# Pooled attention and gated feed-forward: queries of sequences 4 and 5 turned by DMA, eleven late buffers, new orders

## The chip, the cores and the metric

The kernel runs on one core of one Trainium2 chip. The metric is the device time of one execution in microseconds. Before the change it is 210.57 us, the median of three runs (210.29 to 210.69).

## The reference

Eight sequences of 576 tokens, eight heads of 64. Keys and values are averaged over groups of 8 tokens (72 of each are left), queries attend to them, and the result of all heads (512 columns) goes through a gated feed-forward: a product, a convolution of three taps along the tokens, a sigmoid gate, a second product.

```python
k_p = k.reshape(B, H, Sp, pool, D).mean(axis=3)
v_p = v.reshape(B, H, Sp, pool, D).mean(axis=3)
scores = scale * np.matmul(q, k_p.transpose(0, 1, 3, 2))
...
attn = np.exp(scores - max); attn = attn / attn.sum()
x = np.matmul(attn, v_p)            # then (B, S, H * D)
h = np.maximum(x @ w_in, 0.0)
conv_out = sum(conv_w[k] * hp[:, k:k + S, :] for k in range(3))
out = h * sigmoid(conv_out) @ w_out
```

The sums of the second half are shortened here; `scale` is 1/8, `w_in` 512 x 1024, `w_out` 1024 x 512. Inputs and output are float32; the kernel computes in bfloat16 with float32 sums.

## The kernel before

**Work.** The sequences stand in four groups of two: group g holds sequences 2g and 2g + 1. A group's tokens are cut into tiles of 128 rows (tile 4 has 64 of each sequence; group 0 has ten tiles, with 64 rows each of tiles 4 and 9). For each sequence: load queries, keys and values (GpSimd's queue, POOL, which casts float32 to bfloat16 on the way), pool keys and values on VectorE (DVE), turn the keys and the queries so that the head dimension lies on the partitions. For each tile: scores on TensorE (PE, line 608 or 621), maximum (DVE, 634), shift, exponential (ScalarE, ACT, 683), turn of the weights, product with the values (PE, 718), division by the sum (`att_divide`: on ACT eight instructions at line 739, one for each head, or on DVE one at line 746), turn of the result. For each sequence: the first product (`ffn_in`, PE, 776; eight blocks of two halves, each half four matmuls), relu (ACT, 785), the convolution either on PE (940) or as two taps on DVE (912), sigmoid or tanh (ACT), gates (DVE, 990), and the second product for each tile (`ffn_out`, PE, 998; two halves of four matmuls), copied to a buffer (1009) and stored (1021).

**Two ways to turn.** The weights of groups 2 and 3 and the attention results of these groups are turned by a DMA that transposes, issued by SyncE's queue (SP): `att_send` (702, eT<-e) and `att_out` (755, xT<-x). The queries of sequences 0 to 5 are turned on PE: `prep_q`, per sequence two half-turns, either 18 matmuls in the half form (line 542) or 36 in the quarter form (546), and each is copied from PSUM to `qT` by ACT or DVE (560). Where `Q_DMA` names the group (before: group 3 alone), `add_prep_q` instead adds one `q_send` (line 553), a DMA on SP from `qp` to `qT`. Then the keys are laid out otherwise: `turn_keys` (494), once for each sequence, writes the turned keys to both halves of the partitions and `copy_keys` (505) copies them once; in the other groups `turn_pair` (471) turns both sequences' keys together and `copy_pair` (484) copies them in four parts. Scores of a group in `Q_DMA` are always in the quarter form (32 small matmuls, line 608); elsewhere `FORMS` picks that or four full ones (621).

**Order.** Nothing is decided at run time. `Graph.add` makes a list of operations in a fixed sequence of code; `ORDER` lists them by twice their number plus one if the second possible engine takes it, and -1 stands for a fill, a matmul without use. The engines' queues are in this order: each engine takes its own entries one after the other and waits at each for what it needs. So a position in `ORDER` says what is queued behind what. `FORMS` gives the shape of those operations that have two, `PLACES` the buffer or PSUM bank of each use.

**Buffers.** `qT` has three buffers, `qp` (queries as loaded) four, `v` three, `kk` (keys as loaded) one. A load waits until its buffer's last reader is done, and all later loads wait behind it in POOL's queue. The output tiles of group 3 go to "late" buffers: the four `qp` buffers, cut in halves, are read as eight buffers of float32. `add_out` lets their first writer wait until the queries of sequences 4 to 7 are turned:

```python
half_qp = [t.rearrange("p h s -> p (h s)")[:, i * 1024:(i + 1) * 1024] for t in buffers["qp"] for i in range(2)]
buffers["late"] = [t.bitcast(FP32) for t in half_qp]
```

Of the kernel before, what the change touches and what calls it, by code (L numbers as in the profile page):

```python
# [33 lines left out]
class Graph:  # L34
# [23 lines left out]
    Q_DMA = (3,)  # L58
# [14 lines left out]
        0, 16, 4, 24, 12, 44, 28, 8, 10, 14, 32, -1, -1, 42, 36, -1, -1, 40, -1, -1,  # L73
        2, -1, 38, -1, 66, 64, -1, -1, 19, 68, -1, 48, 21, -1, 60, -1, -1, 46, 102, 7,
        26, 34, 114, 118, 106, 116, 121, 108, 104, 113, 111, 122, 126, 125, 292, 128, -1, 74, 30, 294,
        358, -1, -1, 70, 360, 296, -1, -1, 298, 50, 362, 364, 336, 338, 58, 314, 300, 316, 340, -1,
        -1, 342, 130, -1, 318, -1, 344, 320, 132, 380, 303, 134, 322, 382, 347, 194, 196, 136, 384, 201,
        324, 72, 348, 386, 326, 199, 350, 366, 352, 78, 304, 369, 328, 206, 306, 330, 202, 209, 308, 370,
        204, 388, 354, 391, 372, -1, 548, 374, 310, 332, 550, 313, 392, 357, 394, 552, 396, 526, 554, 376,
        528, 398, 335, 570, 556, 401, 572, 530, 226, 532, 558, 574, 379, 228, 230, 576, 504, 444, 506, 84,  # L80
        233, 446, 62, 138, 508, 448, 482, 438, 510, 140, 440, 142, 426, 56, 442, 534, 428, 484, 432, 430,
        144, 434, 537, 52, 486, 76, 512, 488, 420, 436, 422, 514, 80, 560, 54, 424, 516, 402, 562, 518,
        564, 414, 416, 520, 404, 418, 466, 406, 210, 472, 470, 468, 212, 578, 566, 474, 408, 568, 476, 410,
        580, 478, 238, 412, 456, 241, 480, -1, 458, 450, 460, 214, 538, 452, 522, 540, 454, 542, 234, 525,
        462, -1, -1, 237, 582, 216, 262, 221, 584, 464, 82, 225, -1, -1, 219, -1, 223, -1, -1, 265,
        978, 586, 544, 490, 980, 547, 770, 588, 592, 982, 591, 493, 772, 748, 984, 594, 750, 600, 774, 597,
        752, 776, 258, 146, 494, 261, 602, 496, 148, 498, 1000, 605, 934, 608, 1002, 754, 150, 500, 1004, 778,
        503, 610, 936, 781, 756, 152, 613, 624, 759, 154, 626, 614, 86, 1006, -1, 938, 760, 642, 628, 156,
        90, 644, 940, 762, 158, 956, 764, 646, 1008, 942, 958, 94, 1011, 704, 630, 945, 706, 98, 632, 960,
        636, 22, 634, 638, 708, 672, 640, 160, 962, 242, 1012, 96, 676, -1, 782, 674, 986, 1014, 784, -1,  # L90
        88, 1016, 989, 792, 766, 794, 710, 654, 656, 786, 769, 1018, 796, 658, 964, 990, 967, 244, 946, 660,
        1021, 992, 948, 994, 662, 798, 968, 950, 664, 788, 800, 970, 791, 246, 678, 972, 803, 162, 248, 680,
        804, 682, 164, 92, 974, 255, 806, 666, 808, 257, 253, 668, 251, 166, 977, 810, 168, 1186, -1, 670,
        952, 1188, 100, 996, 813, -1, -1, 1190, 999, 694, 955, 170, 1204, 696, 1096, 1206, 1098, 698, 172, 726,
        1192, 1060, 1208, 1100, 1062, 728, 712, 1064, 648, 174, 730, 715, 650, 1090, 176, 652, 1092, 684, 732, 1168,
        688, 1094, 1170, 1104, 1072, 690, 1074, 178, 692, 270, 1076, 1172, 716, 273, 1066, 700, 1194, 1068, 1174, 616,
        1070, 718, 1176, 686, 618, 721, 1084, 180, -1, 702, 1086, 621, -1, 1088, 1150, 1140, 1152, 1210, 1078, 1118,
        1142, 1212, 1080, 1144, 1124, 266, 1082, 1154, 1054, 606, 269, 1102, 1056, 1120, 1196, 1058, 622, 734, 1126, 1428,
        737, 1222, 1198, 830, 1430, 1156, 290, 1224, 1201, 814, 1432, 816, 1226, 1128, 1178, 274, 738, 1122, 832, 819,
        740, 182, 722, 1180, 820, 838, 742, 725, 1182, 835, 744, 840, 1106, 747, 1184, 276, 1410, 843, 1134, 1412,  # L100
        1228, 1158, 884, 1136, 1108, 886, 1138, 1112, 1214, 1230, 888, 878, 1216, 1110, 1414, 880, 1446, 1218, 882, 872,
        1448, 874, 1434, 1220, 918, 278, 876, 1450, 890, 288, 922, 1146, 892, 920, 1160, 894, 846, 1162, 1114, 1165,
        860, 1148, 866, 1436, 868, 1116, 862, 184, 1166, 870, 848, 1130, 864, 280, 1132, 851, 1232, 1202, 283, 284,
        1234, 908, 287, 1236, 1676, 186, 1238, 910, 854, 912, 1678, 1438, 856, 1452, 1440, 836, 1680, 896, 858, 898,
        1442, 1416, 1454, 1640, 188, 902, 900, 1642, 1316, 190, 906, 1644, 1418, 1318, 904, 192, 1392, 1320, 924, 1394,
        1444, 1646, 1322, 1396, 928, 1324, 926, 914, 1280, 1326, 1456, 1398, 1282, 1334, 1458, 930, 1292, 1461, 1400, 1286,
        1288, 1382, 1294, 1648, 1284, 1304, 916, 1296, 1306, 1290, 1462, 1298, 1308, 932, 1300, 1328, 1682, 1402, 1310, 844,
        1302, 1404, 1384, 1312, 1407, 1330, 822, 1336, 1684, 824, 1342, 1314, 1408, 1338, 1604, 827, 1332, 1658, 1420, 1660,
# [1391 lines left out]
```

## Time and profile before

| | |
|---|---|
| median of three runs | 210.57 us (210.29, 210.57, 210.69) |
| the profiled execution | 210.06 us |
| its span, first to last instruction | 208.3 us |
| granted clock of TensorE, mean | 0.993 |
| DMA moved | 33.48 MB, 161 GB/s mean |
| HBM read | 32.52 MB |

The profile is of one execution on the one core. PE is TensorE's matmuls, PEld its weight loads, DVE VectorE, ACT ScalarE, POOL GpSimd, SP SyncE; an engine's name with q is its queue. Groups name a line of the kernel, the output tile and the inputs, the shapes and the count, then busy us, mean ns of one, and the idle time just before them with what ended most of it. The chain of waits is followed back from the last instruction, at each step to what released it; its rows are start, length, and what ran. DMA rows give the issuing queue, the size where it is known, and the median time from issue to landing; queue q0 holds POOL's loads, q1 what SP issues. Rows of a table by stretches give the stretch, its length, then the busy time and number of instructions of PE, PEld, DVE, ACT and POOL, the granted clock, the busy share of the 16 DMA engines and GB/s.

### The profile page before, as it was taken

To read this page: it belongs to the slowest core of one execution; us is meant where nothing else is said; L and a number is where in the kernel's file an instruction comes from. 1 tells how busy PE (TensorE), PEld (TensorE's weight loads), DVE (VectorE), ACT (ScalarE), POOL (GpSimd) and SP (SyncE) were. 2 spreads that over 40 slices of the span, in tenths; PEclk is the share of its full clock that TensorE was granted. 3 is DMA by queue.
4 is the path that set the end of the run, shared out by engine and by line. 5 is a ranking of instruction groups with operands and counts; after the bars stand their busy time and mean duration, and the time that the engine had idled before them with its cause. 6 is when DMAs were issued, how large, how long until landed. Compare 5 with 4: busy or idle time off the path is not lost.

```text
span 208.3 us, 6540 instructions
## 1 busy us (share of the span) xinstructions
PE 197.2 (95%) x2650; PEld 134.3 (64%) x2666; DVE 190.4 (91%) x338; ACT 174.5 (84%) x363; POOL 45.5 (22%) x74
## 2 busy tenths in 40 slices
PE   4999999999999999999999999999999999999990
PEld 2568688776688887666868875566556666644450
DVE  7979999889999999999999999999999999999440
ACT  3558786998899999998998999999999999797310
POOL 8553035010173211010000152040234315000000
PEclk9999999999999999999999999999999999999997
DMA  6999999999999999998497465565665557044395
GB/s 205 243 204 209 205 207 208 208 209 203 189 167 202 205 207 206 170 162 164 92 144 123 97 136 111 119 138 127 129 139 116 120 124 179 3 101 102 92 282 185
DMA packets 48835, 33.48 MB, mean 161 GB/s; under 512 B 28300, under 2 KB 43812, under 8 KB 48804
## 3 DMA queue, kind: packets, MB, share of 16 engines
q0 software_dynamic: 15216, 15.40, 45.1%
q1 hardware_dynamic: 32592, 16.20, 36.4%
q10 hardware_dynamic: 996, 1.45, 2.6%
q8 instruction: 21, 0.34, 0.6%
q14 instruction: 10, 0.08, 0.1%
HBM read 32.52 MB, written 9.44 MB: 201 GB/s over the span
## 4 chain that ended last, share of the span: by engine, by line
PE 49%; DVE 24%; ACT 16%; issue 5%; DMA 3%; SPq 0%; DVEq 0%; ACTq 0%
PE psum L776 19%; PE psum L998 13%; DVE tg L912 6%; DVE negm L634 4%; ACT x L739 4%; PE psum L718 3%; DVE gT L990 3%; DVE sd L646 3%; DMA hT<-in_k_dram 3%; PE psum L940 2%; ACT hT L785 2%; PE psum L693 2%; PE psum L608 2%; ACT gT L922 2%; ACT qT L560 2%
## 5 line engine op out<-in xcount | busy, mean ns | idle before, releaser
L776 PE MATMUL psum<-xT,w_in_sb 128*128 128x288 bf16 x512 | 70.6, 286 | 0.4
L998 PE MATMUL psum<-w_out_sb,gT 128*128 128x512 bf16 (+1 forms) x280 | 65.9, 373 | 1.1 <-issue 0.2
L776 PEld LDWEIGHTS <-w_in_sb 128*128 128x128 bf16 x512 | 48.4, 98 | 15.6 <-issue 0.6
L785 ACT ACTIVATE hT<-psum 128x576 bf16<-128x576 f32 x64 | 41.6, 671 | 4.8 <-PE psum L776 4.2
L998 PEld LDWEIGHTS <-gT 128*128 128x128 bf16 x296 | 27.7, 98 | 27.5 <-DVE gT L990 0.6
L860 POOL COPY hT<-hT 128x126 bf16<-128x126 bf16 x14 | 11.3, 810 | 84.2 <-issue 43.6
L912 DVE SCALAR_TENSOR_TENSOR tg<-hT,ratio 128x576 f32<-128x576 bf16 x36 | 28.2, 813 | 0.5 <-ACT gT L922 0.2
L634 DVE TENSOR_REDUCE negm<-psum 128x8 f32<-128x576 f32 (+2 forms) x37 | 27.4, 748 | 1.3 <-PE psum L608 0.6
L912 DVE SCALAR_TENSOR_TENSOR tg<-hT,ratio,tg 128x576 f32<-128x576 bf16 x36 | 28.2, 810 | 0.0
L922 ACT ACTIVATE gT<-tg,ratio 128x576 bf16<-128x576 f32 x36 | 27.4, 793 | 0.8 <-DVE tg L912 0.7
L990 DVE TENSOR_TENSOR gT<-gT,hT 128x2304 bf16<-128x2304 bf16 x16 | 21.4, 1348 | 0.1
L739 ACT ACTIVATE x<-psum,r 128x64 bf16<-128x64 f32 x96 | 21.2, 356 | 0.1
L1009 ACT COPY osb<-psum 128x512 f32<-128x512 f32 x27 | 16.4, 620 | 4.3 <-PE psum L998 2.7
L646 DVE TENSOR_TENSOR sd<-psum,negm 128x576 f32<-128x576 f32 x27 | 19.8, 747 | 0.1
L683 ACT ACTIVATE e<-sd 128x576 bf16<-128x576 f32 x27 | 19.4, 719 | 0.1
L718 PE MATMUL psum<-vm,eT 128*128 128x65 bf16 (+5 forms) x240 | 18.8, 222 | 0.2 <-DVE vm L516 0.2
L718 PEld LDWEIGHTS <-eT 128*128 128x128 bf16 (+1 forms) x240 | 14.8, 101 | 3.6 <-issue 0.8
L746 DVE TENSOR_TENSOR x<-psum,r 128x512 bf16<-128x512 f32 (+1 forms) x25 | 16.6, 679 | 0.2
L425 PE MATMUL psum<-gT 128*128 128x448 bf16 x40 | 12.7, 425 | 2.8 <-DVE gT L1107 2.8
L940 PE MATMUL psum<-hT,dw 64*64 64x63 bf16 (+2 forms) x448 | 13.2, 255 | 0.2 <-ACT kT L505 0.2
L512 DVE TENSOR_TENSOR v<-v 128x1280 bf16<-128x1280 bf16 (+2 forms) x24 | 12.9, 539 | 0.2
L940 PEld LDWEIGHTS <-dw 64*64 64x64 bf16 x448 | 10.9, 107 | 2.1 <-issue 1.5
(94 smaller groups left out, 236.5 us busy)
## 6 DMA issues: line engine op xcount, KB each, us to landing
out_dram<-osb SPq DMA_DIRECT2D x54, 128.0 KB, 2.4
v<-in_v_dram POOLq DMA_DIRECT2D x8, 512.0 KB, 13.7
qp<-in_q_dram POOLq DMA_DIRECT2D x7, 576.0 KB, 13.2
kk<-in_k_dram POOLq DMA_DIRECT2D x3, 1152.0 KB, 14.4
out_dram<-qp ACTq DMA_DIRECT2D x10, 128.0 KB, 3.4
hT<-in_k_dram SPq DMA_DIRECT2D x2, 576.0 KB, 5.0
w_in_sb<-in_moe_w_in_dram POOLq DMA_DIRECT2D x2, 512.0 KB, 15.4
w_out_sb<-in_moe_w_out_dram POOLq DMA_DIRECT2D x1, 1024.0 KB, 18.6
```

The source lines that it names most:

```text
L634: nc.vector.tensor_reduce(out=a["m"][0:rows], in_=a["s"][0:rows, :, 0:2 * KW].rearrange("p a (h s) -> p a h s", s=Sp), axis=AX.X, op=OP.ma ...
L646: nc.vector.tensor_tensor(out=a["d"][0:rows], in0=a["s"][0:rows, :, 0:2 * KW].rearrange("p a (h s) -> p a h s", s=Sp), in1=a["m"][0:rows]. ...
L683: nc.scalar.activation(out=dst, in_=src, func=ACT.Exp,)
L718: nc.tensor.matmul(out=a["o"][lo:hi, h // 4, (h % 4) * (D + 1):(h % 4 + x1 - x0) * (D + 1)], lhsT=a["eT"][:, j, lo:hi], rhs=buf("vm", b)[: ...
L739: nc.scalar.activation(out=a["x"][0:rows, n * D:(n + 1) * D], in_=ov[:, n // 4, n % 4, 0:D], func=ACT.Identity, scale=r[0:rows, n // 4, n ...
L776: nc.tensor.matmul(out=banks(ps)[:, j, 0:SC], lhsT=w_in_block(dc, fb), rhs=buf("xT", g)[:, dc, i * S + j * SC:i * S + (j + 1) * SC], start ...
L785: nc.scalar.activation(out=h_of(b)[:, fb].rearrange("p (a s) -> p a s", a=2), in_=banks(ps)[:, :, 0:SC], func=ACT.Relu, scale=1.0 if (b, f ...
L912: nc.vector.scalar_tensor_tensor(out=acc, in0=h, scalar=w, in1=acc if tap else mid, op0=OP.mult, op1=OP.add)
L922: nc.scalar.activation(out=gate, in_=acc_of(b, fb, ps), func=squash(b, fb), scale=ratio[:, 1, fb:fb + 1])
L940: nc.tensor.matmul(out=banks(pss[r ^ c])[c * D:(c + 1) * D, j, lo:hi], lhsT=dw[r * D:(r + 1) * D, tap * n_fb + fb, :], rhs=hT[r * D:(r + 1 ...
L990: nc.vector.tensor_tensor(out=gate, in0=gate, in1=h_of(b)[:, four], op=OP.mult)
L998: nc.tensor.matmul(out=bank(ps)[0:rows, columns], lhsT=buf("gT", g)[:, fb, t * P:t * P + rows], rhs=w_out_sb[:, fb, columns], start=(fb == 0),
```

## The change

Group 2 (sequences 4 and 5) is named in `Q_DMA`, so its queries are sent by SP, its keys are turned by `turn_keys` and copied once each, and its scores take the quarter form. Three halves of the `v` buffers are added to the late buffers, and the late buffers' first writer waits for the value sums of sequences 4 to 7 too. `ORDER`, `FORMS` and `PLACES` are new throughout.

```diff
-    Q_DMA = (3,)
+    Q_DMA = (2, 3)
...
     ORDER = (
-        0, 16, 4, 24, 12, 44, 28, 8, 10, 14, 32, -1, -1, 42, 36, -1, -1, 40, -1, -1,
...
+        0, 16, 4, 24, 12, 44, 32, 14, 10, 42, 48, -1, -1, 40, -1, 3, 36, -1, -1, 66,
...
     FORMS = (
-        1, 1, 1, 0, 0, 1, 1, 0, 0, 0, 1, 1, 0, 1, 1, 0, 0, 0, 1, 1, 1, 0, 1, 1, 1, 0, 0, 1, 0, 1, 0, 1, 1, 1, 1, 1, 1, 1, 0, 0,
+        1, 0, 0, 1, 1, 1, 1, 0, 1, 1, 0, 0, 1, 0, 1, 1, 0, 1, 0, 0, 0, 0, 0, 0, 0, 1, 1,
...
-             "hT": 2, "gT": 2, "xT": 2, "qT": 3, "kk": 1, "qp": 4, "v": 3, "vm": 5, "kT": 5, "sd": 3, "r": 3, "s": 2, "late": 8}
+             "hT": 2, "gT": 2, "xT": 2, "qT": 3, "kk": 1, "qp": 4, "v": 3, "vm": 5, "kT": 5, "sd": 3, "r": 3, "s": 2, "late": 11}
...
     half_qp = [t.rearrange("p h s -> p (h s)")[:, i * 1024:(i + 1) * 1024] for t in buffers["qp"] for i in range(2)]
+    half_qp += [t.rearrange("p j x -> p (j x)")[:, 0:1024] for t in buffers["v"]]
     buffers["late"] = [t.bitcast(FP32) for t in half_qp]
...
-            osb, free = (token("late", g, t), [x for n in range(4, B) for x in qdone[n, 0]]) if g == 3 else (token("osb", g, t), [])
+            osb, free = (token("late", g, t), [x for n in range(4, B) for x in qdone[n, 0] + [vdone[n]]]) if g == 3 else (token("osb", g, t), [])
```

What the two orders say when each number is read back to its operation. Positions count from 0; the order before has 1091 entries, the new one 1084.

| operation | before | after |
|---|---|---|
| turning of sequence 4's queries | PE, 246 and 282 | SP, 328 |
| first scores of group 2 | 417 | 409 |
| last scores that read the `qT` buffer of sequence 2 (group 1, tile 1) | 439 | 453 |
| weights sent, group 2 tiles 2 and 1 | 476, 482 | 457, 465 |
| turning of sequence 5's queries | PE, 469 and 505 | SP, 474 |
| first scores that read sequence 5 (group 2, tiles 4 and 7) | 521, 519 | 513, 515 |
| queries of sequences 7 and 6 sent | 526, 589 | 578, 561 |
| first scores of group 3 (tile 4) | 624 | 622 |
| first sum of the last key pair (DVE) | 535 | 490 |
| second step of sequence 6's value sum (DVE) | 487 | 514 |

POOL's loads, before: q0, v0, k1, q1, w_in, q2, v1, w_in, keys 2+3, q3, q4, w_out, v2, v3, keys 4+5, v4, v5, q6, q7, v6, q5, keys 6+7, v7. After: q0, v0, k1, q1, q2, w_in, v1, w_in, v2, keys 2+3, q3, w_out, v3, keys 4+5, q4, v4, v5, q7, v6, q5, keys 6+7, q6, v7. In the new order q7 takes the buffer from which q4 is sent, and v7 stands behind a copy of the edges of h (468) and the end of sequence 5's value sum (496).

Counts by engine, before and after: divisions ACT 12 and 16, DVE 25 and 21; copies of queries ACT 10 and 5, DVE 4 and 5; copies of key pairs ACT 8 and 4; copies of single keys ACT 2 and 4; copies to eT ACT 15 and 16, DVE 4 and 3; copies to xT ACT 18 and 17, DVE 1 and 2; copies of output tiles ACT 31 and 32, DVE 6 and 5; casts of the first loads ACT 3 and 1, DVE 1 and 3. Half-turns of queries of sequences 1 to 3: half form 5 and 2, quarter form 1 and 4. Full scores: 10 and 11. Fills: 40 and 40. Both orders end with five output tiles of group 3 on PE behind the last gate.

144 rows, old and new, of tables (ORDER, PLACES) are left out of this document.

## The prediction

> **What bounds the kernel now.** I read the busy times first, then the work by stage, the chain of waits, the groups, and at last the DMA queues.
>
> ```profile
> PE 197.2 (95%) x2650; PEld 134.3 (64%) x2666; DVE 190.4 (91%) x338; ACT 174.5 (84%) x363; POOL 45.5 (22%) x74
> 28.00:92.00 64.00, 63.24 (x1131) 48.00 (x1135) 61.55 (x116) 58.79 (x109) 14.47 (x26) 1.00 1.19 195
> 92.00:154.00 62.00, 61.25 (x767) 41.23 (x772) 61.62 (x102) 59.91 (x149) 10.14 (x16) 1.00 0.66 127
> 154.00:194.00 40.00, 39.58 (x247) 23.73 (x250) 39.59 (x53) 36.47 (x77) 8.21 (x8) 1.00 0.48 106
> ```
>
> The columns of the last three rows are length, then busy PE, PEld, DVE, ACT and POOL, granted clock, DMA share and GB/s. In none of these stages is PE or DVE idle for over 4%; ACT has 5.2 us to spare from 28 to 92. No engine is the bound alone, so a wait of PE or DVE anywhere in this stretch is not made good later.
>
> ```profile
> 90.38 0.54 PE psum L608 x32
> 91.16 1.29 DVE negm L634 x2
> ...
> 182.80 8.83 DVE tg L912 x12
> 191.63 2.55 DVE gT L990 x2
> 194.23 8.84 PE psum L998 x48
> ```
>
> The chain of waits changes from PE to DVE at 91 us, right behind the first scores that read sequence 5 (tile 7 of group 2, then tile 4). It ends with taps, gates and 48 output matmuls. The new orders end with the same five output tiles behind the last gate, so I count the tail at nothing: its cover is the 48 matmuls, and one more copy of some 0.6 us between the last matmul and its store would show in full.
>
> **The change part by part.** Work first. Durations are of one execution.
>
> ```profile
> 39.52 0.64 PE psum L542 x18
> 81.19 0.41 PE psum L546 x36
> L471 PE MATMUL psum<-pick,kk 128*64 128x64 bf16 x36 | 1.1, 198 | 0.0
> L494 PE MATMUL psum<-ident_k,kk 128*64 128x64 bf16 x36 | 0.9, 197 | 0.0
> ```
>
> PE loses four half-turns of queries in the quarter form: 4 x 0.41 = 1.6 us. Of the turns that remain, three go from the half form (0.64) to the quarter form (0.41): 0.7 less. One turn of a key pair (18 of the 36 matmuls, 0.55) gives way to two turns of single keys (0.45 each): 0.35 more. Sum: 2.0 us less. The scores of group 2 that lose their full form are made up by others of group 1 that gain it, 11 full ones against 10, which I count at nothing: chain pieces of both forms stand at 0.25 to 0.54.
>
> ```profile
> L739 ACT ACTIVATE x<-psum,r 128x64 bf16<-128x64 f32 x96 | 21.2, 356 | 0.1
> L746 DVE TENSOR_TENSOR x<-psum,r 128x512 bf16<-128x512 f32 (+1 forms) x25 | 16.6, 679 | 0.2
> L560 ACT COPY qT<-psum 128x1152 bf16<-128x1152 bf16 (+2 forms) x10 | 10.3, 1025 | 0.3 <-PE psum L542 0.3
> L484 ACT CAST kT<-psum 64x288 bf16<-64x288 f32 x8 | 2.8, 392 | 0.1
> L505 ACT CAST kT<-psum 128x576 bf16<-128x576 f32 x2 | 1.2, 661 | 0.0
> L1009 DVE COPY qp<-psum 128x512 f32<-128x512 f32 (+1 forms) x6 | 3.5, 600 | 5.9 <-PE psum L998 5.9
> L707 ACT COPY eT<-psum 128x640 bf16<-128x640 bf16 (+1 forms) x15 | 9.9, 676 | 0.5 <-PE psum L693 0.3
> L771 ACT COPY xT<-psum 128x512 bf16<-128x512 bf16 (+1 forms) x18 | 9.7, 564 | 1.7 <-PE psum L763 1.5
> L307 ACT CAST qp<-hT 128x512 bf16<-128x512 f32 x2 | 1.1, 619 | 3.7 <-DMA hT<-in_q_dram 3.7
> ...
> out_dram<-osb SPq DMA_DIRECT2D x54, 128.0 KB, 2.4
> ```
>
> DVE loses four divisions (16.6/25 = 0.66 each), 2.7 us; an output copy (0.6) leaves and a query copy of like size comes. ACT gains four divisions, each eight instructions and 21.2/12 = 1.77 us: 7.1 more. It loses five query copies (5.1) and four pair copies (2.8/8 each, 1.4), and gains two key copies (1.2) an eT copy (0.66) and an output copy (0.6), and gives one xT copy (0.54) away. Sum: 2.5 us more on ACT. The casts that change places lie in the first ten us, in the wait for the first transfers (3.7 us by their row), and cost nothing; without that cover they are 1.1 us. I count the three late buffers and the added wait on the values at nothing: they touch only stores of the last group, long after the values are summed. Uncovered, a store's 2.4 us would have to be waited for.
>
> In the stage to 92 us PE can give at most its 2.0 us, and ACT still fits (58.8 + 2.5 into 62.0), though with next to no idle time left. The gain lies between 2.0 and a loss of 2.5 (ACT's addition, if its idle time is all forced by waits). I take 1.6, nearest to PE's side, since PE has the least idle time by the rows.
>
> Now the transfers. The queries of sequence 5 are sent by SP at position 474; tile 4's scores, which need them, are at 513 on PE, and every later matmul is queued behind them, with DVE's maximum of tile 7 next (518). The send cannot go earlier: its qT buffer is sequence 2's, read until tile 1 of group 1 (453), and SP has two sends of attention weights ahead of it (457, 465). What PE has between send and scores:
>
> ```profile
> 57.25 0.98 PE psum L776 x8
> 160.05 0.86 PE psum L998 x4
> 79.35 0.74 PE psum L940 x32
> 73.06 0.38 PE psum L425 x2
> 62.79 0.36 PE psum L718 x6
> 63.15 0.39 PE psum L693 x5
> ```
>
> Seven half blocks of the first product (4 matmuls, 0.49 each), two of the second (0.86), one convolution (0.74), two fills (0.38), one tile of values (0.36) and two small turns (some 0.6): 7.2 us. If the stage gives 1.6 us, tile 4's scores are due at 90.4 - 1.6 = 88.8, and the send stands at 81.6.
>
> ```profile
> qT<-qp SPq DMA_TRANSPOSE x2, 6.1
> L554 SPq DMA_TRANSPOSE qT<-qp x2: 2804/3318/3832, 91.7 to 102.8; - x2
> eT<-e SPq DMA_TRANSPOSE x18, 2.6
> ...
> 82.15 6.36 SPq L702 DMA_TRANSPOSE eT<-e  x3
> ...
> q0 software_dynamic: 591, 0.58, 121.9%
> ...
> eT<-e SPq DMA_TRANSPOSE x2, 6.0
> ...
> q1 hardware_dynamic: 646, 0.16, 127.0%
> ...
> 86.00:87.00 1.00, 1.00 (x49) 0.87 (x48) 1.00 (x2) 1.00 (x3) 0.00 (x0) 1.00 1.01 95
> ```
>
> Idle, such a turn lands in 6.1 us, and 7.2 would do. But both measured ones (91.7 and 102.8) came after the loads, which end about 86 (95 GB/s from there to 87). The 591-packet row is the stretch from 82.5 to 85.4, in which SP had issued two transposes and not one packet of its queue q1 moved; the loads' queue q0 had all the engines. The first of those transposes took 6.0 us in place of 2.6. From 87.2 to 88.0 (the 646-packet row) q1 moved 0.16 MB, 197 GB/s. So I let the transposes wait for the loads. Bytes to load are the same as before, and the gap that the loads have now at 56 to 60 us is replaced by another (sequence 7's load waits for the buffer that sequence 4's send reads, and the rest of POOL's queue waits behind it), so I keep their end at 86. Then come two sends of weights (0.16 MB each) and the queries (128 x 2304 x 2 bytes, 0.59 MB): 0.92 MB at 197 GB/s is 4.7 us. An idle send has 1.2 us before its first packet (the issue row below) and 0.59 MB at 197, 3.0; of 6.1 that leaves 1.9 at the end. Landing: 86 + 4.7 + 1.9 = 92.6.
>
> ```profile
> L702 SPq DMA_TRANSPOSE eT<-e x18: 1200/1237/2061, 82.2 to 161.2; - x18
> 58.00:59.00 1.00, 1.00 (x19) 0.97 (x17) 1.00 (x3) 1.00 (x3) 1.00 (x3) 1.00 0.95 51
> 72.60 0.77 POOL L318 DMA_DIRECT2D v<-in_v_dram  x1 [1.49 <-DVE vm L516]
> ```
>
> The wait at the scores is 92.6 - 88.8 = 3.8 us. From below it is 0 (81.6 + 6.1 = 87.7, in time), from above about 6, if the loads end 2 us later than now. The Trainium skill speaks against my reading: DMA: Bandwidth & Descriptors, section Queues, rings and completion order, says that each engine takes turns between the queues that have work, a packet from each. By it some of q1's packets should have been in the 591-packet row; the trace has none there.
>
> The sequence 4 turn, sent some 58 us, also stands behind loads, but its first scores come 12 us or more later (position 409 against 328): nothing, unless the loads queued behind it run late.
>
> **Sum.** First scores of sequence 5 at 92.6 in place of 90.4: 2.2 later; the 1.6 saved ahead of them is swallowed. Behind them PE has about 0.2 and DVE 0.9 less to do than before, since the last pair's first sum (1.35) is ahead of them now and one value step (0.48) behind; I take 0.4. That is 1.8 over this execution: 208.3 of span and 1.76 around it, 210.06, make 211.9. It lies 0.5 under the median of the three runs, 210.57, so 212.4.
>
> **The rivals.**
>
> *In time, faster.* The queries land before 88.8 and PE never waits: the loads would have to be through by about 82, or q1 to get its packets at once. For it: the idle 6.1 us against 7.2. Against it: the rows of 82.5 to 85.4. The whole saving of 1.6 + 0.4 stays: 208.6. It decides on one number, the landing of sequence 5's queries.
>
> *Turns about.* From 81 on loads (5 us at the 200 GB/s of the 591-packet row, 1.0 MB) and transposes (0.92 MB) share the engines; the transposes, at half of 200, end at 81 + 9.2 = 90.2, land at 92.1 with the 1.9, and it is 1.7 later, less 0.4: 211.9. This is what the rule of the Trainium skill would do here. For it: the rate is the same whoever moves. Against it: that same row with no packet of q1.
>
> *Loads late.* Sequence 4's send waits behind two value loads, sequence 7's load for the send, and everything to the last key pair for that load. If the gap is 2 us longer than the one it replaces (51 GB/s at 58 us now), the loads end at 88 and the queries land at 94.6: 214.4. For it: POOL's queue is in order. Against it: one value load (issued at 72.6 now, 0.59 MB, 2.9 us at 200 GB/s) moves behind the send and makes room.
>
> *ACT the bound.* The queries are in time, but ACT, at 58.8 of 64 us and given 2.5 more, keeps its waits; the saving is lost and the time stays, 210.6.
>
> *Not what it says.* If the queries still turned on PE, the trace would show two sends of queries and not four, and no time would move: 210.6. The diff, which names group 2 beside group 3, speaks against it; I give it nothing.
>
> **How the numbers follow.** Waiting for the loads 0.38 (211.4 to 213.4); loads late 0.12; turns about 0.11; in time 0.33; ACT the bound 0.06. What can be told from no change is 0.2%, 0.4 us. Faster 0.33, same 0.07, slower 0.60. The range for 8 in 10 takes in both signs, from in time to loads late: 208.5 to 214.4.
>
> **What would show it.** Right: one idle stretch of 2 to 5 us on PE between 86 and 95 us whose end is the landing of a qT transpose, with DVE idle just after it; a send of queries between 80 and 84 that takes over 8 us to land; q1 without packets until q0 has drained. The four half-turns gone, 16 tiles of division on ACT, PE with some 2 us less work. Wrong: no such idle stretch, the landing within 7 us, and the first scores of sequence 5 at 89 or earlier, with an end near 208.6. An idle stretch of DVE before the last pair's first sum would point to loads late.

## The result, and the profile after

The changed kernel takes 220.99 us, the median of four runs (219.71 to 222.7), against 210.49 before (210.29 to 210.69, four runs on the same chip): 1.050 times the time, 95% interval 1.042 to 1.059. It is slower, by 10.5 us, and lies outside the range of the prediction (208.5 to 214.4). The profiled execution took 222.7 us, the longest of the four, with a span of 221.0. Medians here and below are of all executions of a kernel, while the ratios leave out those that took over 1.5% longer than its fastest.

The busy times of the page and a table by stretches (columns as before; line numbers are one higher than before from line 253 on):

```profile
PE 200.6 (91%) x2566; PEld 133.9 (61%) x2582; DVE 191.7 (87%) x336; ACT 174.7 (79%) x387; POOL 42.2 (19%) x74
28.00:92.00 64.00, 61.60 (x1044) 46.20 (x1048) 60.38 (x108) 57.95 (x124) 11.15 (x16) 1.00 1.14 188
92.00:104.00 12.00, 5.28 (x67) 3.68 (x66) 5.16 (x9) 4.58 (x10) 2.25 (x4) 0.75 1.32 158
104.00:166.00 62.00, 61.46 (x783) 40.29 (x789) 60.31 (x101) 58.04 (x148) 4.87 (x11) 0.99 0.65 116
166.00:206.00 40.00, 39.57 (x249) 23.93 (x252) 39.20 (x53) 36.26 (x74) 9.93 (x14) 1.00 0.54 114
```

From 104 us on the table reads like that of before. The loss lies ahead: in the twelve microseconds from 92 PE and DVE stand for more than half of the time and the granted clock falls to 0.75, and from 28 to 92 PE and DVE are busy 1.6 and 1.2 us less than in the same stretch before. The chain of waits (start, length, what ran):

```profile
84.66 3.26 DMA eT<-e
87.92 13.87 DMA qT<-qp
...
101.83 0.69 PE psum L609 x23
```

The rows of the waits (us in total, times, longest):

```profile
POOL qp L286 <- DMA qT<-qp: 20.1, 1, 20.1
PE psum L609 <- DMA qT<-qp: 5.9, 1, 5.9
```

The send of sequence 5's queries is issued at 87.92 and its data is there 13.9 us later; PE stands 5.9 us at the scores that read it. The 20.1 us of POOL are the load of sequence 7's queries, which waits for sequence 4's send, with all later loads behind it. The timeline of SP's queue:

```profile
61.52 6.01 SPq L555 DMA_TRANSPOSE qT<-qp  x1
84.66 3.08 SPq L703 DMA_TRANSPOSE eT<-e  x2
87.92 7.90 SPq L555 DMA_TRANSPOSE qT<-qp  x1
```

The DMA queues from 66 to 73 us, from 84 to 88 and from 88 to 92 (packets, MB, share of the 16 engines):

```profile
q1 hardware_dynamic: 2135, 0.77, 57.5%
q0 software_dynamic: 23, 0.02, 1.6%
...
q0 software_dynamic: 802, 0.82, 123.5%
...
q0 software_dynamic: 601, 0.66, 95.4%
q1 hardware_dynamic: 494, 0.13, 23.2%
```

Two rows of stretches after that (the last three columns are the granted clock, the DMA share and GB/s):

```profile
92.00:95.00 3.00, 2.76 (x26) 2.09 (x23) 3.00 (x5) 2.78 (x6) 1.29 (x2) 1.00 1.39 86
97.00:100.00 3.00, 0.00 (x0) 0.00 (x0) 0.00 (x0) 0.00 (x0) 0.00 (x0) 0.69 1.56 98
```

From 84 to 88 the loads (q0) have the engines to themselves though two sends of weights stand issued since 84.66; from 88 to 92 loads and transposes (q1) move about as many packets, but five times as many bytes are the loads'. From 66 to 73 is the hole in the loads behind sequence 4's send: they move 0.02 MB in 7 us. Before, the loads ended about 86; here they still move 0.66 MB from 88 to 92, and the last of them, sequence 7's values, is issued at 93.49. Nor do the transposes get the full rate once the loads give way: from 92 to 95 us all queues together move 86 GB/s, and from 97 to 100, while sequence 7's values start, 98.

### The profile page after: what moved, and what is told of

It reads as the page before. It is cut to its first block, busy times and chain, and to the rows that moved or that the text cites. A ratio compares the mean times of both kernels' runs of the same rounds, so it can differ in the third digit from the quotient of the medians.

```text
span 221.0 us, 6391 instructions
## 1 busy us (share of the span) xinstructions
PE 200.6 (91%) x2566; PEld 133.9 (61%) x2582; DVE 191.7 (87%) x336; ACT 174.7 (79%) x387; POOL 42.2 (19%) x74
## 4 chain that ended last, share of the span: by engine, by line
PE 46%; DVE 19%; ACT 15%; issue 8%; DMA 8%; POOL 1%; POOLq 1%; DVEq 0%; ACTq 0%
PE psum L777 14%; PE psum L999 12%; DMA qT<-qp 6%; DVE tg L913 5%; PE psum L719 4%; ACT x L740 4%; ACT hT L786 3%; PE psum L941 3%; ACT gT L923 2%; DVE gT L991 2%; PE psum L426 2%; PE psum L609 2%; ACT e L684 2%; PE psum L764 2%; DVE negm L635 2%
## 5 line engine op out<-in xcount | busy, mean ns | idle before, releaser
L777 PE MATMUL psum<-xT,w_in_sb 128*128 128x288 bf16 x512 | 71.7, 286 | 0.3 <-ACT hT L786 0.2
L999 PE MATMUL psum<-w_out_sb,gT 128*128 128x512 bf16 (+1 forms) x280 | 67.2, 377 | 2.4 <-DVE gT L991 1.3
L777 PEld LDWEIGHTS <-w_in_sb 128*128 128x128 bf16 x512 | 47.7, 98 | 15.2 <-issue 0.6
L786 ACT ACTIVATE hT<-psum 128x576 bf16<-128x576 f32 x64 | 43.3, 694 | 3.1 <-PE psum L777 2.9
L740 ACT ACTIVATE x<-psum,r 128x64 bf16<-128x64 f32 (+1 forms) x128 | 28.7, 396 | 8.7 <-DVE r L732 8.6
L923 ACT ACTIVATE gT<-tg,ratio 128x576 bf16<-128x576 f32 x36 | 28.7, 841 | 2.8 <-DVE tg L913 2.6
L647 DVE TENSOR_TENSOR sd<-psum,negm 128x576 f32<-128x576 f32 x27 | 20.1, 747 | 0.6
L1010 ACT COPY osb<-psum 128x512 f32<-128x512 f32 x27 | 16.9, 647 | 1.2 <-PE psum L999 0.9
L426 PE MATMUL psum<-gT 128*128 128x448 bf16 x40 | 13.9, 414 | 3.8 <-DVE gT L1108 3.8
L747 DVE TENSOR_TENSOR x<-psum,r 128x512 bf16<-128x512 f32 (+1 forms) x21 | 14.4, 686 | 0.3
L609 PE MATMUL psum<-kT,qT 64*64 64x72 bf16 x392 | 8.3, 206 | 5.9 <-DMA qT<-qp 5.9
```

The costliest lines, as they stand in the source:

```text
L647: nc.vector.tensor_tensor(out=a["d"][0:rows], in0=a["s"][0:rows, :, 0:2 * KW].rearrange("p a (h s) -> p a h s", s=Sp), in1=a["m"][0:rows]. ...
L740: nc.scalar.activation(out=a["x"][0:rows, n * D:(n + 1) * D], in_=ov[:, n // 4, n % 4, 0:D], func=ACT.Identity, scale=r[0:rows, n // 4, n ...
L777: nc.tensor.matmul(out=banks(ps)[:, j, 0:SC], lhsT=w_in_block(dc, fb), rhs=buf("xT", g)[:, dc, i * S + j * SC:i * S + (j + 1) * SC], start ...
L786: nc.scalar.activation(out=h_of(b)[:, fb].rearrange("p (a s) -> p a s", a=2), in_=banks(ps)[:, :, 0:SC], func=ACT.Relu, scale=1.0 if (b, f ...
L923: nc.scalar.activation(out=gate, in_=acc_of(b, fb, ps), func=squash(b, fb), scale=ratio[:, 1, fb:fb + 1])
L999: nc.tensor.matmul(out=bank(ps)[0:rows, columns], lhsT=buf("gT", g)[:, fb, t * P:t * P + rows], rhs=w_out_sb[:, fb, columns], start=(fb == 0),
```

## The experiments

The texts on record name theories by letters. A: most of the loss is the one wait for sequence 5's send. B: the transposes cost their time wherever they stand. C: the loss is the sum of many small delays. D: the turn alone brings most of it. E: the hole in the loads does. F: loads and transposes together move less than in turn. G and H: the new orders cost nothing, or 2 to 3 us. Some letters change their meaning a little from text to text; each text says what its own stands for. Edits of the order are shown as operations with their positions. Each run was measured against the kernel before on the same chip, which took 210.4 to 210.7 there; ratios carry 95% intervals.

**The send early.**

```diff
-  391 POOL load q5    474 SP q_send 5    qT: sequence 5 in 2, 7 in 0
+  269 POOL load q5    354 SP q_send 5    qT: sequence 5 in 0, 7 in 2
```

> The changed kernel, with the load of sequence 5's queries put right behind sequence 5's values in POOL's queue (before sequence 7's queries), and its send moved from behind two sends of probabilities up to right behind sequence 4's send on SP; for that, sequences 5 and 7 swap their turned-query buffers. Theory A (about 6 us of the 10.5 lost are the one wait of the tensor engine for sequence 5's turned queries, 5.9 and 6.0 us in the rows of the waits, and the other 4 to 5 were lost before it): 214 to 216 us, the wait for that send gone from the rows, the lag before 60 us unchanged at about 2 us. Theory B (the transposes cost their time wherever they run, because they and the loads take it from each other): 219 to 222, with a wait of 4 us or more for the query sends, the eT sends or a load in some other place. Theory C (the loss is the sum of many small delays, and the wait only collects slack that would otherwise be lost at the next wait): 218 to 220, the rows of the wait gone but the lag behind 105 us still above 9 us.

Measured: 214.53 us, ratio 1.019 (1.017 to 1.021): 6.5 us of the 10.5 are back, and no row of the waits has PE or DVE waiting for a send of queries. Theory A. The DMA queues from 68 to 76 us:

```profile
q1 hardware_dynamic: 4024, 1.12, 102.7%
q0 software_dynamic: 118, 0.13, 14.8%
```

The waits from 84 to 104 us:

```profile
DVE kk L466 <- DMA kk<-in_k_dram: 1.4, 1, 1.4
PE psum L719 <- DVE sd L647: 1.3, 1, 1.3
```

Both sends of queries are through by about 76 us, since from 68 on they have the DMA engines nearly alone (4024 packets against 118). What is late instead is the load of the last key pair: DVE waits 1.4 us for it, and PE 1.3 us for DVE.

**Sequence 5's send left out.**

```diff
     def q_send(b):
+        if b == 5:
+            return
```

> The changed kernel without the send of sequence 5's queries: its scores read what the buffer held before (so the scores of sequence 5 are not those of its queries), and every load, instruction and buffer else stays where it was. It takes away the wait and the transposes' traffic together. Theory A: 213.5 to 216, about 6 us less than the changed kernel; the difference to the run with the early send is what the traffic of one send of queries costs when it is out of the way, under 1 us. Theory B: here 213 to 215 too, but the early send stays at 219 or more. Theory C: 218 to 220 here as well.

Measured: 213.49 us, 1.015 (1.013 to 1.017). The whole of that send, wait and traffic, is 220.99 - 213.49 = 7.5 us; the early send leaves 1.0 of it. The wait itself is 5.9 of the 7.5. The granted clock, 0.50 from 102 to 104 us, is part of the rest: seven matmuls of the second product, most of what PE does right behind the wait, take 2.71 us there, 0.39 each, where such matmuls take 0.26 in this run (1.04 us for four).

**The start of the kernel before.**

```diff
-  0 to 56: new order and engines of casts, clears, masks, first loads
+  0 to 56: those of the kernel before
```

> The changed kernel with the first 57 instructions (up to the copies of sequence 0's turned queries: casts, clears, masks, the order of the first loads) in the order and on the engines of the kernel before. If the new order of the start costs the 1.5 to 2 us by which the scores' maxima of the changed kernel lag at 11 to 30 us, and nothing later takes them up: 218.5 to 219.5, the lag at 30 us under 0.5 us. If the loads behind it set the stage's pace instead (v1 and w_in landed later), the lag at 30 us stays 1 us or more and the time at 220 to 221. If the wait at 94 us sets the time whatever comes before it, 220 to 221 though the lag at 30 us is gone.

Measured: 223.51 us, 1.058 (1.051 to 1.064): no gain. The maximum of tile 5 of group 0 shows why (timelines of DVE; 30.44 us before). In the changed kernel, in this run, and in the run with the early send:

```profile
31.78 0.75 DVE L635 TENSOR_REDUCE negm<-psum 128x8 bf16<-128x576 f32 x1
```

```profile
30.49 0.75 DVE L635 TENSOR_REDUCE negm<-psum 128x8 bf16<-128x576 f32 x1
```

```profile
30.54 0.75 DVE L635 TENSOR_REDUCE negm<-psum 128x8 bf16<-128x576 f32 x1
```

The run with the early send starts as the changed kernel does, without the lag. The 1.3 us belong to the one profiled execution, not to the order. The start costs nothing.

**The turns alone, in the old order.**

```diff
     Q_DMA = (2, 3)
-  246, 282 PE prep_q 4    469, 505 PE prep_q 5    398 PE turn_pair
+  246 SP q_send 4    465 SP q_send 5    395, 396 PE turn_keys 4, 5
```

> The kernel before with one part of the change alone: the queries of sequences 4 and 5 turned by DMA, their keys on both halves, the scores of that group in 64x64 tiles; each send stands where the first of the two half-turns of its queries stood, and every load stays where it was. Theory A (the turn by DMA is a small gain or nothing where the send is not late; the loss came with the new orders): the tensor engine has 2.0 us less work and the send of sequence 4 is early; for sequence 5 the load stands behind those of sequences 6 and 7 and its send just ahead of the first send of probabilities, so a wait of 0 to 3 us at its scores: 208.5 to 212.5. Theory B (the transposes cost their time wherever they run): 214 or more. Theory D (the turn itself brings most of the loss, by the wait for sequence 5's send): 215 to 218 with a wait of 5 us or more at the first scores of sequence 5.

Measured: 217.47 us, 1.035 (1.031 to 1.040). The turn by itself loses 7 us. Theories B and D both had this time, but the wait that D puts at the first scores of sequence 5 is not there. SP's timeline:

```profile
41.70 9.79 SPq L554 DMA_TRANSPOSE qT<-qp  x1
82.53 6.74 SPq L554 DMA_TRANSPOSE qT<-qp  x1
89.39 6.03 SPq L702 DMA_TRANSPOSE eT<-e  x3
```

Its waits:

```profile
DVE kk L465 <- DMA kk<-in_k_dram: 1.7, 1, 1.7
PE psum L718 <- DMA eT<-e: 2.6, 1, 2.6
```

Sequence 4's send meets loads (its issue takes 9.8 us) and makes the keys of 4 and 5 late; sequence 5's holds up the sends of weights behind it on SP.

**The hole in the loads closed**, first in the changed kernel, then with the early send.

```diff
-  qp: sequence 7 in 2, 6 in 3
+  qp: sequence 7 in 3, 6 in 2
```

> The changed kernel with two buffers swapped and nothing else: the rows of sequence 7's queries go into the buffer that sequence 6 had (free since 30 us), and sequence 6's into the one that sequence 4's send still reads. So the load of sequence 7's queries, and all loads behind it in POOL's queue, no longer wait 20.1 us for sequence 4's send; the stretch from 68 to 76 us in which no load moves closes. Theory E (the sends push the loads back, and late loads then slow the send of sequence 5): loads end at 93 to 97 instead of 103 us, the wait for that send shrinks from 6 to 2 to 4 us, 215.5 to 218.5 us. If the loads' hole costs nothing (only the place of sequence 5's send counts): 219 to 221.

Measured: 220.7 us, 1.039 (1.030 to 1.048). Its four executions lie between 217.47 and 222.62, those of the change between 219.71 and 222.7, so no gain can be told from the spread. But the wait has moved to sequence 4's send, which is issued at 60.30 here and lands 19.95 us later; PE stands 5.0 us at the scores that read it, and no longer at those of sequence 5.

> The early send of sequence 5 and the swapped buffers together. Theory E: in the run with the early send, VectorE waited 1.4 us for sequence 6 and 7's keys at 89.6 us and the tensor engine 1.3 us behind it; with loads that flow through these waits go and the time falls from 214.5 to 211.5 to 213. If that rest of 4 us over the kernel before does not come from the loads (from the divisions on ScalarE, or the new order itself): 214 to 215.

Measured: 223.34 us, 1.057 (1.053 to 1.062), 9 us slower than with the hole. The ranges expected for the run with both end at 215. Theory E, mine, falls: the hole was no damage, it let the sends through.

Two stretches of it, then the DMA queues in the first of them:

```profile
68.00:76.00 8.00, 6.35 (x131) 5.35 (x130) 7.20 (x16) 7.75 (x15) 1.03 (x1) 1.00 1.27 175
76.00:88.00 12.00, 8.18 (x121) 5.83 (x122) 5.25 (x8) 4.16 (x7) 0.77 (x1) 0.72 1.38 96
```

```profile
q0 software_dynamic: 1038, 1.09, 90.2%
q1 hardware_dynamic: 1119, 0.29, 36.3%
```

In the same 8 us (68 to 76) the sends now move 0.29 MB in place of 1.12: packet for packet with the loads, 1119 against 1038. SP is 20.6 us at issuing them instead of 13.1, and PE waits 5.3 us for them.

**Four early divisions back on DVE** (tiles 1, 9, 5 of group 0, tile 3 of group 1), with both cures and with the early send alone.

```diff
-  att_divide: ACT
+  att_divide: DVE
```

> The same as the run with both cures, and four divisions (tiles 1, 9 and 5 of the first pair, tile 3 of the second) back on VectorE. If ScalarE's 1.75 us for each of them holds up the exponentials behind it: 0.5 to 1.5 us less than with both cures. If VectorE's 0.65 us for each weighs as much: the same within 0.4 us, or up to 1 us more.

> The run with the early send, with the four early divisions (tiles 1, 9 and 5 of the first pair, tile 3 of the second) back on VectorE. Theory F (loads and transposes at the same time move less than one after the other, so the hole in the loads is what lets the two sends through; what is left of the loss lies in the new order ahead of 60 us): ScalarE is spared 7 us and VectorE gets 2.6, with both at 7.5 to 7.9 of 8 us there, so 213.5 to 215.0. If the run with both cures lost its 5 us against the run with the divisions moved back to the divisions themselves: 209 to 211 here too. If it lost them to a shift of the loads against the sends: no gain here.

Measured: 218.27 us, 1.036 (1.031 to 1.041) with both cures, and 215.82, 1.024 (1.019 to 1.029) with the early send, where it was 214.53. With the early send alone the four divisions on ACT thus seem worth some 1.3 us to the change, though the two intervals touch. The 5 us gained with both cures, more than any text expected, go with a shorter wait: PE waits 2.3 us for the sends there, in place of 5.3. I take this for a shift of loads against sends, which no run isolates.

**Old order, the turns alone, the send early; and with a hole meant for the sends.**

```diff
-  357 POOL load q5    465 SP q_send 5
+  318 POOL load q5    361 SP q_send 5
```

> The kernel before with the turns by DMA alone, as in the run above that took 217.5 us, but with the load of sequence 5's queries moved ahead of those of 6 and 7 and its send to right behind the scores of tile 4 of the second pair (as in the run with the early send). Theory A (a send that is not late costs little): the wait for probabilities queued behind that send (2.6 us) goes and the time falls to 211 to 214. Theory E (each send, early or late, takes about 5 us of loading from the 80 us in which the loads run without a pause, and whatever load comes last is late by it): the wait turns up at a load instead (keys of 6 and 7, or values of 6 and 7), 213 to 217.

Measured: 220.27 us, 1.045 (1.041 to 1.050), above both expected ranges and worse than with the later send: PE waits 3.4 us for weights, whose three sends take 10.29 us to issue, and DVE 1.6 us each for values and for keys.

```diff
-  159 POOL load q4    328 load q6    334 load q7    348 load v6    357 load q5    401 load keys 6+7
-  246 SP q_send 4    465 SP q_send 5
+  249 POOL load q4    318 load q5    399 load keys 6+7    400 load v6    401 load q7    402 load q6
+  309 SP q_send 4    358 SP q_send 5
```

> The kernel before with the turns by DMA alone, and the loads ordered so that a hole is left for the sends: sequence 4's queries behind the keys of 4 and 5, sequence 5's behind the values of 5, then the keys of 6 and 7 (which wait for the turning of the keys of 4 and 5 on the tensor engine at about 70 us), the values of 6, the queries of 7 and 6. Sequence 4's send then meets loads from 57 to 66 us, sequence 5's send is alone from about 66. Theory F (the two runs with the turns alone lost 7 and 10 us because their sends ran beside loads): 210.5 to 213.5. If the turn by DMA costs its 7 us wherever the loads lie: 216 or more. Under 210: the change could have been a gain, and its new orders lost it.

Measured: 221.47 us, 1.049 (1.044 to 1.055). Theory F had 210.5 to 213.5, but the run did not test it, because the hole did not come in time: the two sends took 24.60 us to issue (from 58.74), and the sends of weights behind them 11.45. Loads ran beside them for most of this, at 167 GB/s for both queues together from 58 to 84 us. From 78 to 84 us they went packet for packet again:

```profile
q0 software_dynamic: 726, 0.73, 86.5%
q1 hardware_dynamic: 726, 0.19, 41.9%
```

**The last keys first**, behind the hole, with the early send; then with the divisions moved too.

```diff
-  377 POOL load q7    382 load v6    413 load keys 6+7
+  411 POOL load keys 6+7    412 load v6    413 load q7
```

> The run with the early send, and behind the hole the loads in another order: the keys of 6 and 7, then the values of 6, the queries of 7, those of 6. No load is then ahead of the keys, for which VectorE waited 1.4 us at 89.6 us and the tensor engine 1.3 us behind it; they should land at about 84 us in place of 91.0. Theory F: 212.5 to 213.8. If that wait is only where slack collects: 214 to 215. If the loads, all moved behind the turning of the keys at 75 us, are now late for the queries of 7 and 6: 215 to 218.

> Both edits of the two runs above on the run with the early send. Theory F: 212 to 213.8, the sum of the two gains. If one of the two loses, the same as the better one of them plus that loss.

Measured: 213.44 us, 1.016 (1.011 to 1.020), and DVE's wait of 1.4 us for keys is no longer in the rows; with the divisions on DVE 216.16, 1.027 (1.021 to 1.033), 2.7 us more, where Theory F had 212 to 213.8.

**Neither send**, in the new and in the old order.

```diff
     def q_send(b):
+        if b in (4, 5):
+            return
...
-                            lhs = buf("qT", b)[rows, m // 2 * P + f * TB:m // 2 * P + (f + 1) * TB]
+                            lhs = (buffers["qT"][0] if b == 4 else buf("qT", b))[rows, m // 2 * P + f * TB:m // 2 * P + (f + 1) * TB]
```

The second edit is in the new order alone.

> The changed kernel without the sends of the queries of sequences 4 and 5 (the scores of these two read what the buffers held, so they are not those of their queries). Wait and traffic of both sends are gone, the loads flow through, the new orders stay. Theory G (the new orders cost nothing, all of the loss is the DMA work of two more sends): 208 to 210, as my forecast had it for turns in time. Theory H (the new orders lose 2 to 3 us ahead of 92 us, whatever the sends do): 212 to 213.5.

> The kernel before with the turns alone (the run that took 217.5 us), without the sends of sequences 4 and 5 (their scores read what the buffers held). What is left is the tensor engine's 2.0 us less of work and the copies saved, with no transposes beside the loads. If the saved work is worth what the sum said: 208.3 to 209.5. If it is worth nothing where two engines share the bound: 210 to 211. If the 64x64 scores and the keys turned twice cost more than the turns save: 211 to 213. The difference to 217.5 us is what the two sends' traffic costs in the old order.

Measured: 212.66 us, 1.009 (1.007 to 1.011) in the new order, 211.16, 1.003 (1.001 to 1.005) in the old. Even with every transpose of theirs gone neither is faster than before. So the loss comes apart: 2.0 us from the new order with the turns' work taken out (212.66 against 210.66 on that chip), 0.8 from sequence 4's send (213.49 - 212.66), 7.5 from sequence 5's; 10.3 in all, the rest of the 10.5 being the difference between the runs of before. In the old order the two sends cost 217.47 - 211.16 = 6.3. The stretch from 44 to 60 us without sends, and the kernel before in the same stretch:

```profile
44.00:60.00 16.00, 14.88 (x211) 10.23 (x203) 15.34 (x24) 15.40 (x40) 5.17 (x7) 1.00 1.23 205
```

```profile
44.00:60.00 16.00, 15.69 (x274) 10.76 (x276) 15.87 (x29) 14.63 (x25) 4.69 (x7) 1.00 1.16 186
```

PE is busy 0.8 us less and DVE 0.5 less here. In the old order without sends:

```profile
28.00:92.00 64.00, 62.73 (x1024) 47.30 (x1023) 61.27 (x114) 55.13 (x101) 15.18 (x27) 1.00 1.22 192
```

ACT is 3.7 us lighter than before, PE 0.5, DVE 0.3, and no time comes of it.

**Without 17 of the fills**, with the early send and the keys first.

```diff
-  -1, 17 times between 200 and 560
```

> The best version so far (early send, keys of 6 and 7 first: 213.4 us), without the 17 fills that its order has between 36 and 90 us (matmuls without use; from 12 to 92 us fills take 9.1 us of the tensor engine in the run without sends, and 6.9 in the kernel before). If the fills hold up work behind them: 211 to 212.5. If they only cover waits, as idle time would: 213 to 214, with that much more idle time of the tensor engine. If the clock falls without them: more than 214 and a granted clock under 0.99.

Measured: 213.07 us, 1.011 (1.009 to 1.013), a granted clock of 0.994. The fills cover waits and cost at most some tenths, as the intervals of the two runs overlap. This is the fastest version of the change that computes everything; the kernel before stays ahead of it.

**The late buffers alone**, in the old order, whose tiles 1, 0 and 5 of group 3 shared one.

```diff
-  late: group 3 tile 0 in 5, tile 5 in 5
+  late: group 3 tile 0 in 8, tile 5 in 9
```

> The kernel before with the eleven late buffers alone (three more in the buffers of the values, two of the last group's tiles moved to them, which had shared one buffer with a third). By the forecast, nothing: 210.2 to 210.8. If the sharing held up the end (ScalarE's wait of 4.8 us for a store at the end): 208 to 210.

Measured: 210.68 us, ratio 0.9996 (0.998 to 1.001): nothing, as forecast.

**The traffic alone.** Eight loads of queries, then four sends, then six loads and four sends together.

> The traffic by itself, nothing of the reference is computed: eight loads of a sequence's queries (0.59 MB written each, as in the kernel) one behind the other; then four sends of turned queries from one buffer; then six such loads and four such sends started together. Theory F (mixed, both get slower than in turn): loads alone 2.8 to 3.0 us each (205 GB/s in the rows of the kernel before), sends alone 4 to 6 us each; six loads and four sends mixed take over 1.2 times the sum of what they take alone (over 45 us by the middle of these). If they only share one rate: 0.95 to 1.1 times the sum. If they run beside each other: the longer of the two.

The queues in 15 us of loads alone, in 9 us of sends alone, and in 15 us of both:

```profile
q0 software_dynamic: 2783, 3.11, 121.2%
...
q1 hardware_dynamic: 7377, 1.86, 111.7%
...
q0 software_dynamic: 2152, 2.41, 92.7%
q1 hardware_dynamic: 2152, 0.54, 27.5%
```

The same three stretches, with GB/s as the last column:

```profile
10.00:25.00 15.00, 0.00 (x0) 0.00 (x0) 1.00 1.21 208
29.00:38.00 9.00, 0.00 (x0) 0.00 (x0) 1.00 1.12 207
45.00:60.00 15.00, 0.00 (x0) 0.07 (x1) 1.00 1.20 197
```

And 2 us while the last loads give way to the sends, then 2 us of the last sends alone:

```profile
65.50:67.50 2.00, 0.00 (x0) 0.00 (x0) 1.00 1.30 80
68.00:70.00 2.00, 0.00 (x0) 0.00 (x0) 1.00 1.27 270
```

Alone, either moves 207 to 208 GB/s, and the last sends 270. Together they share 197, and they share it by packets: 2152 and 2152. A load's packet holds 2.41 MB / 2152 = 1120 bytes, a transpose's 0.54 / 2152 = 250. So beside loads a send gets 36 GB/s, and by that its 0.59 MB would take 16 us in place of 2.9. Theory F, that both together move much less, is not what the 15 us together show; they share a rate, in unequal parts. In the kernels the total did fall (175 and 96 GB/s with both cures, 167 in the run with a hole meant for the sends), and here it fell to 80 where the loads ran out; why, no run shows.

The second run of this kind, with keys and values beside the sends:

> Traffic by itself again, nothing of the reference is computed: loads of queries, of pairs of keys and of values alone, then two loads of key pairs and four of values started together with five sends of queries. In the first run of this kind loads of queries and sends took turns packet by packet (2152 packets each in 15 us). If that holds for the other loads too, their counts are equal here as well, and the total stays near 200 GB/s. If keys or values beside sends are what brought the run with both cures to 96 GB/s from 76 to 88 us, the total falls to about 100 GB/s here.

The 3 us from 31.6, while the second send starts, and the 14.5 us from 35.5:

```profile
q0 software_dynamic: 478, 0.49, 115.6%
q1 hardware_dynamic: 5, 0.00, 0.3%
...
q0 software_dynamic: 2252, 2.26, 91.6%
q1 hardware_dynamic: 2245, 0.57, 30.0%
```

The turns are equal for keys and values too. But this send, started beside loads, moved almost nothing for 3 us first. It is not so at every start: in the first of these runs one send ends and the next begins between 45 and 60 us, and the counts stay equal.

## Why the prediction was wrong

**The place and the kind of the wait were right.** I forecast one idle stretch of PE behind the send of sequence 5's queries, at the scores of tiles 4 and 7, and from it a slower kernel. The rows of the waits and the chain show it, and the run without that send is 7.5 us faster.

**The step that failed is the end of the loads, "I keep their end at 86", and with it the landing at 92.6.** Measured: issue at 87.92, landing at 101.8. I took the transposes' bytes as traffic that comes after the loads and leaves them as they are. But sequence 4's send runs in the midst of the loads; they all but stop from 66 to 73 us behind it and are still moving at 92; by then 0.13 of the 0.92 MB of transposes had moved. **The rate behind the loads was wrong too.** I had 4.7 us for 0.92 MB at 197 GB/s. The last 0.79 MB took until about 100 us, 8 us in place of 4, at 86 GB/s from 92 to 95 and with the last 0.08 MB beside sequence 7's values from 97 on. Of the 9.2 us that the landing came late, some 6 are thus the loads' end and some 4 the rate, less 0.7 for the 0.13 MB moved before 92. The rival "loads late" had the first of the two, with 12% and a price of 2 us: the mechanism right, the price too small.

**"I let the transposes wait for the loads"** was half right. In the row of before without a packet of q1 a send was, as I read it now, only starting: the run with keys and values shows that pause as 3 us beside loads. After it the queues do take turns. The Trainium skill, in DMA: Bandwidth & Descriptors, section Queues, rings and completion order, says that each engine takes turns between queues by the packet; 2152 against 2152 agrees. My rival "turns about" halved the rate by bytes. By packets of 250 and 1120 bytes the send's part is 0.54 of 2.95 MB, a fifth to a sixth, so a send that has loads beside it all the time would take 16 us, where the rival let all transposes end 9.2 us after 81.

**The term "I take 1.6"**, the gain of the stage to 92 us, came out as a loss. The bounds were +2.0 and -2.5; without sends the new order stands at -2.0. The half-turns did leave PE, by the groups of the changed kernel:

```profile
L543 PE MATMUL psum<-ident,qp 128*64 128x128 bf16 x72 | 3.5, 244 | 0.6 <-DVE qp L308 0.6
L547 PE MATMUL psum<-ident,qp 64*64 64x64 bf16 x144 | 2.1, 195 | 0.1
```

5.6 us in place of the 7.1 of before (4.6 and 2.5). But with work of PE saved in the old order nothing was gained either (211.16). That PE and DVE share the bound would explain it; the busy times fit, but no run shows it as the cause. Where the 2.0 go is shown only in part: 0.8 us of PE from 44 to 60. It is hardly "ACT the bound": with four divisions moved back to DVE the time rose by 1.3 and 2.7 us in the runs with the early send, and fell only where both cures let the sends meet the loads.

**The wait** was put at 3.8 us and measured at 5.9, at the upper bound that I had given ("about 6"). The wait by itself was thus sized within its bounds, but by luck: the landing was 9.2 us late and PE came to it 7 us late, at 95.9 us (101.8 - 5.9) and not at 88.8. The first scores that read sequence 5, before, in the new order without sends, and without sequence 5's send (PE's timelines):

```profile
90.31 0.58 PE L608 MATMUL psum<-kT,qT 64*64 64x72 bf16 x32
...
92.82 0.47 PE L611 MATMUL psum<-kT,qT 64*64 64x72 bf16 x32
...
93.95 0.45 PE L611 MATMUL psum<-kT,qT 64*64 64x72 bf16 x32
```

So 4.0 of the 7 us (92.82 - 88.8) are the new order itself, 2.5 us later than before where I had 1.6 earlier. Sequence 4's send adds 1.1, and of the last 2 us some 1.3 are the one execution's own.

**"Nothing, unless the loads queued behind it run late"** for sequence 4's send: 0.8 us when it is the only one. **The tail** and **the late buffers**, both at nothing, held: the stretch from 166 us reads as before, and the late buffers alone made 0.9996. **The casts** of the start at nothing held too. **"In time"** fell as a rival twice over: the queries landed late, and even with no send at all the time is 212.66, not 208.6.

## What to carry to other kernels

A transfer moved to the DMA queues competes with every load that runs then, and the queues share by packets, not by bytes: a transpose of 256-byte packets beside loads of 1.1 KB gets a fifth to a sixth of the rate. Either give such transposes a stretch without loads (here a load that waits for the buffer of the send made one, and closing it cost 9 us with the early send) or leave the work on the engine. And before counting a saving on one engine, look whether a second engine is as busy: some two microseconds less of PE were worth nothing here.

## What the runs showed of the hardware

- Loads and transposes together move 197 GB/s, with equal counts of packets, 2152 and 2152 or 2252 and 2245, where either alone moves 207 to 208 over 9 to 15 us. The Trainium skill, in Advanced Engine Details and Errata, section X-Bar Transpose (TRN2), has transposing DMAs as fast as regular ones, and alone they are. The same section of the Trainium skill expects 350 to 400 GB/s; here they moved 207, and 270 in 2 us at the end.
- A transposing DMA that started beside running loads moved 5 packets in 3 us (478 of the loads in the same time) before the turns became equal; a send that began between 45 and 60 us in the other run of the traffic had no such pause.
- Where PE was busy 5.28 and 8.18 of 12 us, the granted clock stood at 0.75 and 0.72 (92 to 104 us after the change, 76 to 88 us with both cures). After the change it was 0.50 from 102 to 104 us, when PE was at work again.
- Open: with both cures the DMA queues moved only 96 GB/s from 76 to 88 us at a busy share of 1.38, in the changed kernel 86 from 92 to 95 at 1.39, and in the first run of the traffic alone 80 for 2 us at 1.30, when the loads ran out beside a send. Equal turns do not explain this, and no run shows what does.
